# Plain matmuls for tokens 2048 to 2559, masks per key block, and V rows copied on the chip, in a fused attention and MLP kernel

## The chip, the cores and the metric

The kernel runs on one core of one Trainium2 chip. The core has five engines that run side by side: TensorE (PE, matmuls; PEld is its weight load), VectorE (DVE), ScalarE (ACT), GpSimd (POOL, here only a queue that issues DMAs and one iota) and SyncE (SP, a queue for DMAs). They meet through semaphores alone. The metric is the device time of one execution in microseconds; lower is better.

## The reference, cut to what matters

Attention with a sliding window of 32 tokens to each side, for 8 batches, 8 heads, 576 tokens and head size 64. Its output, turned to 4608 tokens by 512 features, goes through a two-layer network with squared ReLU:

```
scores = scale * np.matmul(q, k.transpose(0, 1, 3, 2))
mask = np.abs(pos[:, None] - pos[None, :]) <= 32
scores = np.where(mask, scores, -1e9)
attn = exp(scores - max); attn = attn / sum(attn)
x = (attn @ v).transpose(0, 2, 1, 3).reshape(4608, 512)
h = x @ w_in            # 512 x 2048
g = maximum(h, 0) ** 2
out = g @ w_out         # 2048 x 512
```

## The kernel before, in words

**Attention** works in 24 groups of 192 queries, three for each batch (G = 3 * batch + g). POOL loads q, k and v for a group with casting DMAs (lines 377 and 415). For the first nine groups PE turns q and k (line 463) and DVE or ACT copies the result out (477, 476); for the later ones a transposing DMA on SP does it (491). A group has two key blocks of 128 keys, A and B. For each, PE makes the scores of all heads (531), ACT takes the exponential of 128x1024 (554), DVE multiplies by the 0/1 mask of the window (562), and PE multiplies by V (590), whose 65th column of ones gives the row sum. DVE takes the reciprocal (604) and scales (608) into `xa` and `xb`; the part of the accumulator that block B starts alone is zeroed on ACT (614) or DVE (615). PE (630, 636) or a DMA turns `xa` and `xb` into `xt`.

Key block A of a group begins 32 keys ahead of its 192 tokens, block B 128 later, so the last 64 rows of block B of one group are the first 64 rows of block A of the next group of the batch. The function `load_v` either loads such rows twice, or copies them from one V buffer to the next on DVE (line 410) or ACT (412):

```
if self.vcopy(G) and j == 0:          # vcopy: G % 3 > 0 and G >= VC
    lo += 64
    vs, vf = self.V[(G - 1) % NV][64:128, 1, :, 0:64], vt[0:64, 0, :, 0:64]
    self.p.rec("DVE", lambda e, vs=vs, vf=vf: e.tensor_copy(vf, vs), reads=[("v", (G - 1) % NV, 1)], ...
```

The masks are multiplied for both key blocks in one instruction of 2048 elements where `MP` is 1 and a group's scores were recorded together (groups 6 and up), else for each block in one of 1024. `NPT` is the number of 128x1024 buffers for masked exponentials.

**The first layer** works on tiles of tokens: four of 192, one of 256, then seven of 512 from token 1024 on. A tile of 512 is made in one of two ways. `mm1` is plain: 16 products, each of four matmuls of 128x512 (line 690), then a ReLU from PSUM (665 on ACT, 664 on DVE) and a square (660 on DVE, 659 on ACT) into `gt`. With the tile in `PAIR`, two products share one ReLU and one square of 1024. `mm1s` is Strassen's scheme: seven instead of eight block products, four times 28 matmuls of 128x256 (line 770), with four differences of `xt` (742) ahead of them, and for each quarter a seeding copy in PSUM (809, 810), two copies out (670, 669), two additions (794), a ReLU (800, 801) and squares. A Strassen group may need one more PE matmul that clears its bank (line 895; marked with a w in the second part of `ORDER`, below). `MM1S` lists the tiles made so.

**The second layer** is plain for the first 512 tokens (835) and Strassen's for the rest (line 917, sums on DVE at 885, additions at 949). Outputs leave by DMAs from ACT and SP (847, 848).

**What sets the order.** Every operation is recorded with its reads and writes. A table, `ORDER`, gives each operation its engine and its place: the program is sorted by these numbers and written out, one strict sequence for each engine, with semaphore waits where data crosses engines. A second part of the table gives buffers and PSUM banks. Where PE's sequence has room ahead of token 0's first layer, `fill` puts matmuls on zeros (line 299), which nobody reads.

Of the kernel before, what the change touches and what calls it, by code (L numbers as in the profile page):

```python
# [21 lines left out]
    MM1S=(2048, 2560, 3072, 3584, 4096),  # L22
# [9 lines left out]
    PAIR=(1536,),  # L32
# [9 lines left out]
    MP=1,  # L42
    S34=1,
    NZ=0,
    VC=99,
# [4 lines left out]
    NPT=4,  # L50
# [182 lines left out]
class Gen:  # L233
# [7 lines left out]
    def alloc(self):  # L241
# [733 lines left out]
    def record(self):  # L975
# [81 lines left out]
        at(4.0, self.sums_w2, 4.0)  # L1057
        if cfg["MM1S"]:
            at(4.5, self.sums_w1, 4.5)
# [26 lines left out]
D900 G1350 A129696 D1800 D9508 D10128 D10418 D10688 D7198 D9088 D12405 D8968 D7698 D8398 D9408 D7398 D2020 D9308 D7818  # L1086
D8108 D17412 D9928 D12805 D13710 D7498 D9708 D12605 D17302 D8683 D14866 D23833 D17702 D39949 S900 D4366 S1350 D6598
G1700 G2488 G4852 G4064 G5640 G3276 G8840 G7216 A900 A13271 A1350 A6839 G6428 G9580 G7956 G10464 G11348 G12128 G14580
G15360 G17756 G16140 G12908 G13792 G18536 G19316 P7268 A7873 P8308 A8860 P9765 A10400 D11719 P10190 A11428 D13025
P12475 D13910 D14180 D14966 P15634 D16146 D16416 P15114 P17172 A17612 P10615 D11167 P11225 A12456 P13361 A13996 D15461  # L1090
P13786 A15024 D18507 P16216 D17102 D17822 A18577 P19276 D19746 D20016 P19536 P20851 D21291 P15344 A16867 P14211 A16052
P17665 A19186 D21843 P20426 A21061 D24619 P22598 D23081 D23933 A25450 P26388 D27094 D27364 P24838 P28702 D30325 G20932
G21768 G20096 G16920 G24920 G29504 P41968 D42573 P40496 A41308 P43262 A43897 D45015 P18517 D22528 P43687 A45477 D46595
P19766 A23151 A24140 P45774 D46386 D47280 D48036 P49140 D49610 D49880 P51114 P51344 D51838 P21081 A23646 P23518 D25304
A27788 P26648 A28603 P27308 A29188 D29773 P29592 D34242 G23392 G22604 G27188 G27976 G43361 G45917 P45432 D48531 P47354
A47906 P28042 D34864 A35487 P49400 A50035 D51153 P24178 D25856 P51574 A52352 D53470 P25068 A26479 A29683 P52442 D53127
D54155 D54911 P55806 D56291 D57177 P57386 P58583 D59595 P21913 D23281 D33556 D38025 D37340 D38711 D35969 D45700 D43192
D57862 P22858 A24955 A26974 P25728 D30878 D26409 D32871 D28050 D36654 D28735 D40069 D31430 D32185 P30912 A32202 A32787
P30252 A31122 G26448 G28764 G24180 G25708 G46801 G48521 P47696 D49083 P47986 A49216 P28932 A31707 A36301 P50689 A51324
D52442 P31572 D35417 P51999 A53380 D55406 P44772 A47399 A57337 P55546 D56091 D56491 D58548 P59473 D60148 D60900 P58011  # L1100
P62644 D63084 P36348 D40754 P46034 A46904 A55037 P33960 D39396 P34620 P37008 P38736 P40891 A42229 A59141 P42363 A43233
D50565 P44112 A44982 G45081 G44245 G52653 G47685 G59793 G63781 P57616 A59521 P59733 A60443 P46694 A48721 D64189 P61994
A62994 A64112 D65507 P52702 A55852 P54886 A56842 A62179 P67289 D67759 D68029 A68941 P73039 D73509 D73969 P74079 P75183
A75994 P33096 P35484 P37872 P39632 A40706 A94765 P56066 A58646 P58813 D60348 A61364 P54226 A56347 P56726 A58152 D75340
P60992 D63636 G51029 G42573 G55017 G54229 G58121 G50145 P58241 D59043 P61652 D62204 P32232 P48276 P49825 P53362 A54436
S113850 P76293 A78955 A80051 P65775 A66795 A67913 D69031 P68422 A69549 P71033 D71620 D71890 D72645 P73299 D73769
D74655 P73849 P75413 D75893 P67549 A70240 D70934 P63738 D64821 P64611 A65695 D70249 P60128 P62874 P66425 P69295 A70842
A129316 P71293 A72376 G67125 G57381 G53489 G55805 G65453 G59005 P73559 A74059 P65485 D66725 P74309 A75393 D77130
G56545 G51817 G62945 G49309 G64665 G87303 P75643 A76809 A77927 D79045 S69616 S68326 P70159 A71443 P81919 D82389 D82659
A83760 P84769 D85318 D85588 P103901 P105644 D106314 P72166 A73249 D76445 P77816 A79450 D80263 D86274 D83345 D88177  # L1110
D84100 P85893 P86767 A87851 P89154 P94023 D99960 D95953 A104236 P90288 P91162 D92246 P97154 P98891 A99975 P94897
P102153 D104943 S139197 P101279 P103027 D106866 A116182 P105874 P106748 A107832 A121814 P79543 D80948 A81704 P82179
A85997 P85029 A86689 A95145 G61369 G66337 G60581 G62157 G79875 G75935 P81269 A82732 A84368 D86959 S67036 S71616 P76953
D78026 P90028 D93131 D93401 A94157 P96634 D99005 D99275 S94157 S100030 P83906 A85396 D88863 P80406 D81634 P83043
D89548 A96173 P78679 A80866 P98028 D101178 D101934 G77607 G68701 G69441 G78347 G86419 G104247 P87641 A88501 A89619
D90737 S83639 S91003 P92296 D96638 P92036 D92931 D94087 D95458 P96894 D97364 D97634 S102530 S101280 P95771 A97394
D98319 P88291 A90647 P93159 D94772 D105628 P99765 A103635 P104781 A107159 D108769 G75099 G80759 G84699 G67865 G76819
G100393 P100629 A101489 A102607 D103725 S95407 S92293 P115980 P117103 A118177 A122194 D102619 D116722 D111687 D117608
D112915 P114232 P115106 A116562 P118227 P119101 D120503 A120185 S128302 P121098 P124573 D125657 P122835 P126960
A130126 P127834 P128708 D132956 S140937 P133035 P135657 D136741 S137497 P133909 P134783 A135867 A145085 P108272  # L1120
D109455 D109725 A110480 P111985 D112455 D114133 S112600 S123182 P119975 P121972 D123292 D124580 P112505 P113369
A114442 D121921 G79087 G83911 G83123 G82335 G85535 G107255 P104131 A105013 A106131 D107551 S88423 S96697 P110259
P111122 A112195 A120786 P112245 D112715 D114819 A115574 P117967 D118437 D119322 S115574 S120642 P131309 P132172
A133245 A134363 P108532 P109395 D110469 D131165 G74359 G105775 G81595 G106515 G113703 G108975 P107622 A108839 A111088
D115504 S89713 S111310 P123709 P125447 D128729 D134746 P116843 D117408 D118637 D120008 P120838 D121721 D122606 S119392
S137947 P129582 P130445 A131519 D134060 D132536 D133641 D126840 D135431 P136531 A137178 P138055 D138702 A140576
P138492 D139388 P139820 A141177 P140517 D141869 P142702 D143772 A148131 D155834 P143399 A145465 A150362 P137618
A139974 P140954 A143077 D154996 P142265 A143678 P143836 A144483 P145147 D145794 P145584 D146691 D148062 D149699
P146718 A147530 A151565 P146281 A146928 P148029 A149159 A155866 P150651 D151298 P151348 A152167 P152222 D152939
P153096 D154310 D155415 A156467 P153970 A155264 A160153 P148466 A149761 P151785 A152768 A153460 P152659 D153625  # L1130
P153533 A154663 P155281 D156557 P158116 D159103 D162111 D164054 P159427 A160754 A161446 D128044 D131851 D135851
D140073 D137427 P138946 P141391 A142475 P144273 P147155 D148482 A150964 S154259 P148903 P149777 A154061 P154407
P155718 A158523 P157242 P158553 D159788 S160544 P159864 P161388 D163369 S164124 P162262 P163136 A164220 S190571
G109763 G110599 G90491 G108139 G111435 G134127 P126310 A127170 A128288 D129947 S124432 S125722 P140257 D140759 D141029
A141784 P143139 D144458 D144728 S146733 S145483 G116259 G117047 G117835 G99605 G133243 G140625 P136968 A137828 A138946
D142554 S130042 S128752 P146021 D146491 D147377 D150385 P151088 D151984 D152254 S150563 S153009 G112223 G112963
G105035 G103507 G160271 G141509 P156592 A157495 A159125 D160474 S127012 S121892 P164447 D164917 D165187 A166025
P167766 D168462 D169359 S165943 S185090 D158684 D161692 D162950 D162530 P164010 A164822 P165581 A166633 D180492
P166018 D167091 P167329 A167976 P168026 D168673 P168900 D170044 D172948 A175430 P169774 A170421 A173626 P164707
A165423 P166455 A168578 D176379 P166892 A169781 P169337 A172334 P170648 D173367 P174664 D175693 A177060 D182129  # L1140
P174227 A176458 D187961 P165144 A167234 P168463 A169179 A174829 P170211 A171023 P171085 A171732 P171782 D176798
P176849 D178169 D180073 A181534 P184751 A185398 A186601 P179684 A180331 P181869 A182562 A188976 P182566 A183213
# [80 lines left out]
```

## Time and profile before

| | |
|---|---|
| three runs, median (lowest to highest) | 288.12 us (288.11 to 289.0) |
| the profiled execution: its own time | 288.54 us |
| its span, first to last instruction | 286.7 us |
| busy: PE, PEld, DVE, ACT, POOL | 98%, 81%, 82%, 70%, 41% |
| instructions: PE, DVE, ACT | 3097, 424, 302 |
| moved by DMA | 38.62 MB, 171107 packets |

Busy PE is the union of matmuls in flight. A matmul lasts longer than the next one waits for it, so PE counts as busy while it only runs slower; the time from one matmul's start to the next tells more, and the chain of waits shows it as the length of a run of matmuls. In the page "out<-in" names the tile written and the tile read; "x" is a count.

### The profile page before, as it was taken

The page shows a single profiled execution, that of the slowest core. Times are in us where ns is not written, and L with a number is a line of the kernel's source. Part 1 is how long each engine was busy: PE and PEld are TensorE (multiplying, and loading weights), DVE is VectorE, ACT ScalarE, POOL GpSimd, SP SyncE. Part 2 cuts the span into 40 slices and gives each one's busy share as a digit, 9 for nine tenths or more (in the row PEclk, how much of TensorE's full clock was granted, in tenths as well). Part 3 has the DMA queues.
Part 4 walks back from the last instruction along what each step waited for, and adds up shares of the span by engine and source line. Part 5 has one row for each costly group of instructions (what it writes and reads, how often), then busy time and mean ns, then how long its engine had stood idle before and what let it go on. Part 6 is the DMA issues. An engine that isn't in the chain of part 4 may idle for free.

```text
span 286.7 us, 7639 instructions
## 1 busy us (share of the span) xinstructions
PE 280.1 (98%) x3097; PEld 232.0 (81%) x3115; DVE 236.0 (82%) x424; ACT 201.7 (70%) x302; POOL 117.9 (41%) x153
## 2 busy tenths in 40 slices
PE   8999999999999999999999999999999999999995
PEld 8979858787857775776898898988888888888884
DVE  2779968878898988979889889899999989979631
ACT  1777638887795476636878899888887768776520
POOL 8999109998693269403702994310000000000000
PEclk9999999999999999999999999999999999999999
DMA  9999999999999999999999999998720431102123
GB/s 147 157 192 204 205 161 148 144 158 148 162 141 150 182 148 143 194 163 186 135 195 158 144 162 155 134 189 137 148 53 13 134 87 40 37 2 71 41 91 130
DMA packets 171107, 38.62 MB, mean 135 GB/s; under 512 B 158272, under 2 KB 170560, under 8 KB 171072
## 3 DMA queue, kind: packets, MB, share of 16 engines
q0 software_dynamic: 121920, 18.98, 94.4%
q1 hardware_dynamic: 43344, 14.30, 29.0%
q10 hardware_dynamic: 5808, 4.85, 5.5%
q8 instruction: 25, 0.41, 0.6%
q14 instruction: 10, 0.08, 0.1%
HBM read 38.80 MB, written 9.44 MB: 168 GB/s over the span
## 4 chain that ended last, share of the span: by engine, by line
PE 93%; DVE 3%; ACT 2%; issue 1%; ACTq 0%
PE ps L917 34%; PE ps L770 22%; PE ps L690 19%; PE ps L835 5%; PE ps L590 4%; PE ps L531 4%; PE ps L299 3%; PE ps L463 2%; ACT e L554 1%; PE ps L630 1%; DVE pt L562 1%; PE ps L636 1%; DVE xa L608 0%; ACT oe L670 0%; DVE xb L608 0%
## 5 line engine op out<-in xcount | busy, mean ns | idle before, releaser
L690 PE MATMUL ps<-xt,w 128*128 128x192 bf16 (+2 forms) x438 | 60.9, 286 | 0.7 <-issue 0.3
L670 ACT ACTIVATE oe<-ps 128x512 f32<-128x512 f32 x62 | 36.0, 596 | 29.4 <-PE ps L917 16.6
L554 ACT ACTIVATE e<-ps 128x1024 bf16<-128x1024 f32 x48 | 48.6, 1021 | 11.0 <-PE ps L531 8.9
L665 ACT ACTIVATE rt<-ps 128x512 bf16<-128x512 f32 (+2 forms) x76 | 44.0, 594 | 16.7 <-PE ps L690 9.6
L377 POOL DMA_DIRECT2D raw<-in_k_dram x46 | 36.4, 810 | 35.9 <-DMA kq<-raw 21.7
L690 PEld LDWEIGHTS ps<-xt,w 128*128 128x128 bf16 x448 | 38.7, 98 | 13.8 <-DVE xt L646 0.3
L377 POOL DMA_DIRECT2D raw<-in_q_dram x46 | 36.9, 815 | 27.3 <-DMA kq<-raw 26.5
L917 PE MATMUL ps<-w,gt 128*128 128x256 bf16 x384 | 47.3, 273 | 0.0
L659 ACT ACTIVATE gt<-rt 128x512 bf16<-128x512 bf16 (+2 forms) x56 | 43.2, 793 | 2.6 <-DVE rt L664 1.8
L415 POOL DMA_DIRECT2D v<-in_v_dram x48 | 42.0, 887 | 6.1 <-PE ps L590 6.1
L917 PEld LDWEIGHTS ps<-w,gt 128*128 128x128 bf16 x384 | 36.8, 98 | 6.0 <-issue 0.6
L562 DVE TENSOR_TENSOR pt<-e,mask 128x2048 bf16<-128x2048 bf16 (+1 forms) x30 | 30.3, 1009 | 3.9 <-ACT e L554 3.5
L770 PE MATMUL ps<-xs,sw 128*128 128x256 bf16 x240 | 32.7, 272 | 0.0
L917 PE MATMUL ps<-ts,gt 128*128 128x256 bf16 x256 | 31.7, 273 | 0.0
L917 PE MATMUL ps<-ts,ss 128*128 128x256 bf16 x256 | 31.4, 273 | 0.0
L794 DVE TENSOR_TENSOR rt<-ps,oe 128x512 bf16<-128x512 f32 x40 | 27.3, 687 | 4.0 <-PE ps L770 3.2
L917 PEld LDWEIGHTS ps<-ts,ss 128*128 128x128 bf16 x256 | 24.4, 98 | 3.7
L917 PEld LDWEIGHTS ps<-ts,gt 128*128 128x128 bf16 x256 | 24.7, 98 | 3.1
L770 PEld LDWEIGHTS ps<-xs,sw 128*128 128x128 bf16 x240 | 23.0, 98 | 2.6
L660 DVE TENSOR_TENSOR gt<-rt 128x1024 bf16<-128x1024 bf16 (+2 forms) x40 | 23.3, 590 | 0.5 <-ACT rt L665 0.4
L770 PE MATMUL ps<-xt,w 128*128 128x256 bf16 x160 | 22.1, 273 | 0.1
L664 DVE TENSOR_SCALAR rt<-ps 128x512 bf16<-128x512 f32 (+2 forms) x28 | 19.0, 685 | 2.1 <-PE ps L690 1.3
(69 smaller groups left out, 389.9 us busy)
## 6 DMA issues: line engine op xcount, KB each, us to landing
out_dram<-oe SPq DMA_DIRECT2D x19, 256.0 KB, 3.0
out_dram<-oe ACTq DMA_DIRECT2D x17, 256.0 KB, 2.5
v<-in_v_dram POOLq DMA_DIRECT2D x32, 128.0 KB, 5.7
w<-in_moe_w_in_dram POOLq DMA_DIRECT2D x4, 512.0 KB, 9.6
w<-in_moe_w_out_dram POOLq DMA_DIRECT2D x4, 512.0 KB, 16.7
raw<-in_q_dram POOLq DMA_DIRECT2D x18, 96.0 KB, 5.3
raw<-in_q_dram POOLq DMA_DIRECT2D x14, 112.0 KB, 4.9
raw<-in_k_dram POOLq DMA_DIRECT2D x14, 112.0 KB, 4.6
```

The lines of the kernel that those rows point to most:

```text
L377: self.p.rec("POOL", lambda e, j=j, dst=dst: e.dma_start(dst, s[j]), writes=[self.rtag(t, b, g, j)], dma=(f"{t}{G % self.cfg['NRAW']}{j}", ...
L415: self.p.rec("POOL", lambda e, j=j, lo=lo, hi=hi, k0=k0: e.dma_start(vt[lo - k0:hi - k0, j, :, 0:64], self.v[b, :, lo:hi, :].rearrange("h ...
L554: last = self.p.rec("ACT", lambda e, ef=ef, v=v: e.activation(ef(), self.bank(v, 0, 2), ACTF.Exp, scale=0.125), reads=[v], writes=tags, ke ...
L562: self.p.rec("DVE", lambda e, pf=pf, ef=ef, mb=mb, n=n: e.tensor_tensor(pf(y=0, n=n), ef(y=0, n=n).rearrange("p (w h q) -> p w h q", w=n, ...
L659: alt = ("ACT", act(c), lambda e: e.activation(dst, src(), ACTF.Square)) if self.cfg["ALT"] else None
L660: self.p.rec("DVE", lambda e: e.tensor_tensor(dst, src(), src(), ALU.mult), reads=rd, writes=wr, key=key, dur=dve(c), name=name, alt=alt, ...
L665: return self.p.rec("ACT", lambda e: e.activation(dst(), src(), ACTF.Relu), reads=rd, writes=wr, key=key, dur=act(c), name=name, alt=alt, ...
L670: self.p.rec("ACT", lambda e: e.activation(dst(), src(), ACTF.Copy), reads=rd, writes=wr, key=key, dur=act(c), name=name, alt=alt, bias=se ...
L690: mm = e.matmul(ht[:, n * x:n * x + n], self.W1[:, ft, 128 * d:128 * d + 128], self.XT[:, ft, r:r + n], start=(ft == 0 and x == 0), stop=( ...
L770: mm = e.matmul(bk[:, 256 * x:256 * x + 256], lhs(k, 256 * m + 128 * x), rhs[:, k, :], start=start and x == 0 and k == 0, stop=(k == 1), s ...
L794: add.append(p.rec("DVE", lambda e: e.tensor_tensor(hs(), src(), self.oe(u), ALU.add), reads=[tg, u], writes=[(hh, y)], key=kk, dur=dve(51 ...
L917: mm = e.matmul(op[:, 256 * y:256 * y + 256], lhs[:, l0[0] + k, a:a + 128], rhs[:, r0 + k, c0:c0 + 256], start=start and y == 0 and k == 0 ...
```

## The change

Five settings change, and with them the whole table `ORDER`:

```diff
-    MM1S=(2048, 2560, 3072, 3584, 4096),
+    MM1S=(2560, 3072, 3584, 4096),
...
-    PAIR=(1536,),
+    PAIR=(),
...
-    MP=1,
+    MP=0,
...
-    VC=99,
+    VC=0,
...
-    NPT=4,
+    NPT=3,
...
 ORDER = """
-D900 G1350 A129696 D1800 D9508 D10128 D10418 D10688 D7198 D9088 D12405 D8968 D7698 D8398 D9408 D7398 D2020 D9308 D7818
+D900 G1350 A131953 D1800 D9496 D10301 D10591 D11011 D2305 D9981 D12979 D2505 D8173 D9696 D10201 D9396 D7888 D19226
...
```

Tokens 2048 to 2559 leave Strassen's scheme: 112 matmuls of 128x256 go, 64 of 128x512 come. Tokens 1536 to 2047 take one ReLU for each product. The 18 masks of 2048 become 36 of 1024. Sixteen groups (all that are not the first of their batch) get the first 64 rows of key block A by a copy on the chip, ten on DVE and six on ACT; 16 of the 32 V loads of 128 rows become loads of 64. One buffer for masked exponentials goes, and one of the two bank-clearing matmuls.

On DVE, at the start of the program, the rows from the scaling of the first group's block A (`xa0`) to that of the second group's (`xa1`). Before:

```order
L608 TENSOR_TENSOR xa0<-ps,rs0 64x512 [waits s_DVE]
L345 MEMSET v3 128x16x2
L615 MEMSET ps 64x2x260 [waits s_DVE]
L562 TENSOR_TENSOR pt<-e,mask 128x1024 [waits s_ACT]
L604 RECIPROCAL rs1<-ps 128x8 [waits s_PE]
L608 TENSOR_TENSOR xb0<-ps,rs1 128x512 [waits s_DVE]
L604 RECIPROCAL rs2<-ps 64x8 [waits s_PE]
L329 MEMSET mask 32x64
L293 MEMSET xa2 64x256
L293 MEMSET kq1 128x4x16
L608 TENSOR_TENSOR xa1<-ps,rs2 64x512 [waits s_DVE]
```

The same stretch of DVE in the changed kernel; `d_v01` is the landing of the V load from which the copy reads:

```order
L608 TENSOR_TENSOR xa0<-ps,rs0 64x512 [waits s_DVE]
L562 TENSOR_TENSOR pt<-e,mask 128x1024 [waits s_DVE,s_ACT]
L562 TENSOR_TENSOR pt<-e,mask 128x1024 [waits s_ACT]
L410 COPY v1<-v0 64x8x64 [waits d_v01]
L604 RECIPROCAL rs1<-ps 128x8 [waits s_PE]
L608 TENSOR_TENSOR xb0<-ps,rs1 128x512 [waits s_DVE]
L604 RECIPROCAL rs2<-ps 64x8 [waits s_PE]
L608 TENSOR_TENSOR xa1<-ps,rs2 64x512 [waits s_DVE]
```

The zeroing of PSUM went to ACT, four memsets went elsewhere, one mask that stood ahead of this stretch came in, and the first V copy stands between the masks and the reciprocal.

On PE, where the second batch begins, the turns of its first k and q (128x112), the first scores (531) and what stands around them. Before:

```order
L835 MATMUL ps<-w,gt 128x512 x16
L463 MATMUL ps<-ident,raw 128x112 x8
L835 MATMUL ps<-w,gt 128x512 x4
L463 MATMUL ps<-ident,raw 128x112 x8
L690 MATMUL ps<-xt,w 128x192 x8
L531 MATMUL ps<-kq 128x128 x16
L690 MATMUL ps<-xt,w 128x192 x16
```

The same place on PE in the changed kernel:

```order
L690 MATMUL ps<-xt,w 128x192 x16
L463 MATMUL ps<-ident,raw 128x112 x8
L690 MATMUL ps<-xt,w 128x192 x8
L463 MATMUL ps<-ident,raw 128x112 x8
L690 MATMUL ps<-xt,w 128x192 x16
L531 MATMUL ps<-kq 128x128 x8
L835 MATMUL ps<-w,gt 128x512 x8
```

The scores come apart into single blocks, and between the second turn and the first scores stand sixteen matmuls of 128x192 where eight stood.

On PE, the beginning of tokens 2048 to 2559. Before, with Strassen's products of the first layer at line 770:

```order
L917 MATMUL ps<-w,gt 128x256 x8
L770 MATMUL ps<-xt,w 128x256 x4
L531 MATMUL ps<-kq 128x128 x16
L770 MATMUL ps<-xt,w 128x256 x8
L770 MATMUL ps<-xs,sw 128x256 x4
L917 MATMUL ps<-w,gt 128x256 x8
L770 MATMUL ps<-xs,sw 128x256 x4
L590 MATMUL ps<-v,pt 128x65 x8
```

The beginning of the same tokens on PE in the changed kernel:

```order
L917 MATMUL ps<-ts,gt 128x256 x8
L690 MATMUL ps<-xt,w 128x512 x8
L531 MATMUL ps<-kq 128x128 x16
L917 MATMUL ps<-w,gt 128x256 x8
L690 MATMUL ps<-xt,w 128x512 x12
L590 MATMUL ps<-v,pt 128x65 x8
L690 MATMUL ps<-xt,w 128x512 x4
L917 MATMUL ps<-w,gt 128x256 x8
```

Plain products of 128x512 stand where the Strassen products stood, mixed with the same second-layer products (917), scores and V products.

More of the change, by code (lines that the diff above doesn't have):

```diff
@@ L1091 @@
[L1091 to L1105, printed above, removed]
@@ new lines @@
+P152548 D153875 D155030 S167444 S170536 P152808 A153881 A162216 D155716 D157553 D160029 D164165 P166821 A167633
+P168829 A169476 D170884 P168392 D170199 P170577 A171281 P172325 D173259 P172762 D176005 D182112 D182951 P178089
+D179842 A186974 P167258 A168234 P169266 A170078 A175633 P169703 A170679 P171014 A171882 P171451 D172574 P173199
+D173945 D175586 D179087 P173636 A174430 D182531 P167955 A168836 P171888 A172535 A173227 P170140 A173828 P174333
+A175031 P174770 D176690 P176081 D177446 A178901 D180528 P177652 A178299 A188177 P180924 A181571 P182495 A183802
@@ new lines @@
+A187575 P183806 A184453 P185117 A185764 P185554 D186456 P186865 D188735 D189840 A190673 P188436 A189380 A190071
+D161819 D162794 D164585 D168295 D168981 P175207 P176518 A177602 P180050 P181361 D185207 A183201 S183892 P178526
+P182932 A185055 P184243 P185991 A188778 P187302 P188873 D190259 A199741 P189747 P192145 D196209 A197557 P191271
+P193669 D196895 A200729 G115945 G123133 G127025 G115109 G153272 G151504 P149026 A149886 D151004 A150914 D152375
+S137173 S131019 P152288 D154075 D154345 A155346 P156272 D157353 D159343 S173036 S176866 G118357 G127861 G125449
@@ new lines @@
+G124661 D162504 G161604 G152388 P157406 A158266 D161133 A159294 D160448 S138463 S144099 P164813 D165283 D165553
+A166328 P167695 D171303 D171573 S171786 S179406 G150024 G163920 G150764 G158548 A176842 G157856 G169532 P160667
+A165300 D167610 A164272 D166924 S155577 S169246 D187827 D188316 D189421 D191145 P194543 A195190 P196745 A197937
+A206129 P197182 A199140 P199190 D199907 P200064 D201277 P200938 D202648 A205101 D207017 P202249 A203061 D205912
+P197879 A198538 P199627 D201963 A209895 P200501 A201148 P202718 D203365 P203415 D204251 P205163 D206331 D207702
@@ new lines @@
+D210980 P206297 A207332 A225747 P203852 A204499 P205600 A206730 A211707 P206734 A207933 P208045 A208692 P208919
+D210295 P210667 D211666 D213753 A214962 P211541 A212910 A215990 P208482 A209294 P210230 A212308 D213334 P211104
+D212648 P213112 A213759 P213549 D215277 P215734 D217357 D219148 A219756 P216171 A217098 D227552 D187141 D200592
+D192249 D197580 D193620 P194997 P195871 A196955 P198316 P201375 D208121 A202459 A203662 P204289 P209356 A210497
+P207171 P212238 A214361 P213986 P214860 D215963 A216718 P219006 P219880 D226866 S227622 P217258 P218132 A220784
@@ L1190 @@
+0 5 4 1 6 1 6 0 3 5 2 5 2 3 2 0 4 3 1 2 3 0 4 2 0 1 1 2 4 2 1 2 0 0 0 1 1 4 3 0 0w 1 0 2 4 7 2 6 5 4 2 1 6 0 3 2 2 7 4
+6 5 4 4 7 6 3 1 5 0 4 2 0 4 0 1 1 0 0 3 0 4 2 1 0 0 2 4 2 1 6 0 0 4 4 0 0 1 1 5 6 3 2 7 0 4 4 2 4 6 1 5 2 1 4 1 0 5 4
+1 2 6 0 5 1 3 2 5
 """
```

158 lines of the change are left out of this document (75 added, 83 removed), and 11 rows, old and new, of the table ORDER.

## The prediction

> **What bounds the kernel now.** I read the page first: busy shares and the 40 slices.
>
> ```profile
> span 286.7 us, 7639 instructions
> PE 280.1 (98%) x3097; PEld 232.0 (81%) x3115; DVE 236.0 (82%) x424; ACT 201.7 (70%) x302; POOL 117.9 (41%) x153
> PE   8999999999999999999999999999999999999995
> PEclk9999999999999999999999999999999999999999
> ```
>
> PE is busy from the first slice to the last, at the full granted clock. Then I asked what PE waits for, and how much of each stretch it is busy (the windows; the columns are PE, PEld, DVE, ACT, POOL, each with its count).
>
> ```profile
> PE ps L299 <- DVE zz L293: 1.2, 1, 1.2
> PE ps L590 <- ACT e L554: 0.4, 1, 0.4
> PE ps L690 <- issue: 0.3, 2, 0.2
> PE ps L590 <- ACT ps L614: 0.2, 1, 0.2
> PE ps L835 <- issue: 0.2, 1, 0.2
> ```
>
> ```profile
> 0.00:20.00 20.00, 18.46 (x297) 17.04 (x298) 11.89 (x43) 11.94 (x15) 19.05 (x29) 1.00 1.63 164
> 40.00:60.00 20.00, 19.24 (x286) 15.89 (x287) 15.06 (x29) 16.23 (x25) 17.06 (x22) 1.00 2.25 146
> 60.00:140.00 80.00, 79.05 (x812) 56.57 (x821) 68.48 (x110) 53.06 (x69) 46.54 (x60) 1.00 1.76 160
> 140.00:260.00 120.00, 119.89 (x1288) 105.46 (x1288) 108.70 (x189) 98.50 (x158) 25.37 (x32) 1.00 0.96 111
> 260.00:286.70 26.70, 23.47 (x216) 20.73 (x213) 13.52 (x20) 10.36 (x18) 0.00 (x0) 1.00 0.26 90
> ```
>
> Apart from the start, PE's waits that have a name come to 1.1 us. The windows give the room that is left: 0.76 us without a matmul in 40 to 60, 0.95 in 60 to 140, 0.11 in 140 to 260. So the change moves the time by PE's own work, by the start (where most of PE's time goes to matmuls on zeros), and by these small gaps. What it saves on DVE, ACT or in DMA counts only where PE waits for it.
>
> **The change part by part: PE's work.** The chain of waits gives the pace, since a run of matmuls in it has the length that the next one waited for.
>
> ```profile
> 113.02 1.73 PE ps L690 x8
> 246.79 8.73 PE ps L770 x80
> ```
>
> The 128x512 runs at 1.73 / 8 = 0.216 us, the 128x256 at 8.73 / 80 = 0.109. The plain tile costs 64 x 0.216 = 13.82 us, Strassen's 112 x 0.109 = 12.22: **+1.6 us**. One bank-clearing matmul of 128x512 goes: **-0.22**. Both bounds are close, since nothing else in the chain is so regular.
>
> The Trainium skill speaks to this in "TensorE: Matmul & The Clock Gate", section "Back-to-back issue gap": it gives 131 ns for a matmul of 512 columns in a sustained stream and 81 for 128, and calls 216 the isolated figure. This trace has 216 in a stream, so it does not agree; by that rule the plain tile would cost 8.4 us, which is a rival below.
>
> **The start.** Until the first layer begins, PE follows DVE.
>
> ```profile
> 8.47 0.56 PE ps L299 x10
> 14.03 0.69 DVE xa L608
> 15.06 0.49 DVE ps L615
> 17.55 0.11 DVE mask L329
> 17.77 0.27 DVE xa L293
> 18.05 0.09 DVE kq L293
> 18.15 0.71 DVE xa L608
> L562 DVE TENSOR_TENSOR pt<-e,mask 128x1024 bf16<-128x1024 bf16 x12 | 8.3, 691 | 1.7 <-ACT e L554 1.4
> L394 DVE CAST raw<-ts 112x512 bf16<-112x512 f32 x2 | 0.9, 428 | 4.2 <-DMA ts<-in_k_dram 4.2
> L664 DVE TENSOR_SCALAR rt<-ps 128x512 bf16<-128x512 f32 x13 | 8.9, 687 | 1.3 <-PE ps L690 0.7 <-ACT e L554 0.3
> ```
>
> Between the two scalings (14.03 to 18.15) the change takes out the zeroing and three memsets, 0.49 + 0.11 + 0.27 + 0.09 = 0.96 us, and puts in a V copy. No copy from SBUF to SBUF stands in the trace; the nearest row is the cast of 512 elements, 0.43, and a read from PSUM, 0.69, bounds it above. Net -0.53 (-0.27 at the upper bound). The mask that comes in (0.69) stood just ahead of this stretch before, so it moves the first scaling forward by as much. A second reading: the program carries 148 matmuls on zeros where it carried 161, and ten take 0.56, so 13 fewer are 0.73 us of room that the new order does not have. I take **-0.7**, with bounds 0 (the DVE chain is not what ends last) and -1.0 (all that goes, and the copy is hidden). The cover for the first copy is the V load: it must have landed when DVE arrives.
>
> **Where the second batch begins.**
>
> ```profile
> 42.57 0.64 DVE kq L477
> 46.04 1.32 PE ps L690 x16
> 51.47 1.03 ACT e L554
> ```
>
> The first scores of batch 1 waited for the copy of the turned k (0.64), with eight matmuls of 128x192 between them and the turn; now sixteen stand there, 1.32 us, which covers the copy. The exponential at 51.47 stood in the chain because a V product (590) had only scores (531) just ahead of it; in the changed order second-layer matmuls (835) stand there. Together they make the 0.76 of this window: I take **-0.5**, bounds 0 and -0.76. To hide this the changed order needs the loads of k and q of batch 1 earlier than before; they share POOL's queue with the weights, and if one lands late the wait comes back here.
>
> **Late stretched runs.**
>
> ```profile
> 174.82 0.91 PE ps L770 x8
> 197.51 2.34 PE ps L770 x20
> 205.22 0.60 PE ps L770 x4
> ```
>
> At 0.109 these should take 0.87, 2.18 and 0.44: 0.36 us together, in products that waited for DVE or ACT to empty a bank while PE counted as busy. The order there is new; I take **-0.3**, bounds 0 and -0.4.
>
> **Masks, pairs, copies, buffers.**
>
> ```profile
> L562 DVE TENSOR_TENSOR pt<-e,mask 128x2048 bf16<-128x2048 bf16 x18 | 22.0, 1221 | 2.2 <-ACT e L554 2.1
> L794 DVE TENSOR_TENSOR rt<-ps,oe 128x512 bf16<-128x512 f32 x40 | 27.3, 687 | 4.0 <-PE ps L770 3.2
> L665 ACT ACTIVATE rt<-ps 128x1024 bf16<-128x1024 f32 x5 | 5.1, 1023 | 5.9 <-PE ps L690 5.9
> ```
>
> Masks: 18 x (2 x 0.691 - 1.221) = +2.9 us of DVE. Copies: ten on DVE, 4.3 at 0.43, six on ACT. Strassen's eight additions go, 8 x 0.687 = -5.5, and some ReLUs move over from ACT. DVE comes out about even and stays near 82%, ACT near 70% (a ReLU of 1024 takes 1.023, two of 512 a little more); PE's matmuls hide all this. If that cover is gone, each instruction costs PE its own length, 0.4 to 0.7. With three buffers for masked exponentials instead of four, a mask may wait for the V product of three blocks earlier: nothing, unless PE is late. The sixteen shorter V loads relieve DMA, and no wait of PE above is for a DMA: nothing.
>
> What is new is a wait of DVE and ACT for a landing, in the middle of the program.
>
> ```profile
> POOL raw L377 <- DMA kq<-raw: 48.2, 8, 13.8
> L415 POOL DMA_DIRECT2D v<-in_v_dram x4: 777/849/930, 106.6 to 112.9; - x4
> DMA to landing us min/median/max: 4.3/5.2/6.2
> L377 POOL DMA_DIRECT2D raw<-in_k_dram x8: 721/833/872, 105.2 to 116.1; - x8
> DMA to landing us min/median/max: 4.2/5.5/7.2
> ```
>
> The four rows after the first are the V loads and the k and q loads of 105 to 120, a burst of issues after POOL had waited for buffers (48.2 us in eight such waits). In it a landing takes 4.2 to 7.2 us. Behind a held copy stand, on DVE, the mask of the next block and the reciprocals and scalings, and on ACT exponentials and ReLUs; PE waits for those with V products and free banks. The 24 groups hand work over between ACT, DVE and PE now at a cost to PE of 0.4 + 0.2 us, about 0.025 for a group; sixteen copies at half that are **+0.2**, bounds 0 and +1.4 (below).
>
> The Trainium skill has a rule against such copies: "SBUF — State Buffer", section "Who interferes with whom", says that a DVE copy with both ends in SBUF can enter a mode in which GpSimd is locked out until it ends, and the descriptors of POOL's DMAs are written by GpSimd. No run here shows it; in the burst above POOL issues a V load in 0.78 to 0.93 us with DVE 86% busy (68.48 of the 80 us around).
>
> Even a POOL held for ten copies of 0.43 us loses 4.3 of the 48.2 us that it waits anyhow, so I count nothing for that.
>
> **Sum.** +1.6 - 0.22 - 0.7 - 0.5 - 0.3 + 0.2 = +0.1 us, on a profiled execution of 288.54 (span 286.7 and 1.84 around it). That run lies 0.4 above the median, 288.12, of which two runs lie within 0.01; the terms are differences, so they go onto the median: **288.2 us**. A measurement here tells about 0.3%, 0.86 us, from no change.
>
> **The rivals.** *A V copy holds DVE or ACT.* A copy that meets a landing of 7.2 instead of 5.2 us holds its engine by up to 2.0 us; a bank that is emptied in 0.69 lets PE run on for about that long. Two held copies of which 0.7 us each reaches PE give +1.4, 289.6. It decides from the second such copy on. For it: DVE is 82% busy and strictly in order, and the loads come in bursts. Against it: there are five V buffers, and V loads ran ahead of use far enough that PE waited for none. Chance 0.18.
>
> *The gaps stay.* If the start and the small gaps are latencies that any order has, only the sum of work counts: 288.12 + 1.6 - 0.22 + 0.2 = 289.7. For it: 0.95 us of gaps in 60 to 140 are spread over many handovers. Against it: the two at 43 and 52 have names, and what named them moved. Chance 0.12.
>
> *The gaps all close.* Start -1.0, second batch -0.76, late -0.4, half of the 0.95 as well, no new wait: 1.6 - 0.22 - 2.6 = -1.3, 286.8. For it: masks of one block let the first V product start 0.53 us earlier (1.221 - 0.691) in every group. Chance 0.11.
>
> *Wide matmuls come cheaper than narrow ones.* With 512 columns at a pace well under 216 ns, say 131, and 256 at 98 (between 81 and 131), the tile would cost 8.4 against 11.0, -2.6 instead of +1.6: 284.0. The page on TensorE would have it so; the chain's runs speak against it. Chance 0.02.
>
> *The change doesn't do what it says:* the V rows are saved, but PE did not wait for them. That is part of the forecast, not a case beside it.
>
> **How the numbers follow.** The forecast, within 0.3% of before, has 0.57; the two slower rivals 0.30 together, the two faster 0.13. The forecast's own range is 287.3 to 289.0. To leave out no more than 2 in 10, the range goes up to 289.7, which takes in both slower rivals at their price, and down to 287.2: the faster rivals, 0.13, stay outside, and so does what is slower than priced.
>
> **What the changed profile would show.** The first layer's first matmul (690) some 0.6 us earlier than before; no DVE copy of a turned k in the chain near 43; runs of 690 at 0.216 in tokens 2048 to 2559, without gaps; DVE and ACT without a wait for a V load, or with short ones that no PE wait follows. I would be wrong if DVE shows waits of 1 us or more for V loads (first rival), if the windows 40 to 60 and 60 to 140 still lack 1.5 us together (second), or if the end comes late by something not in this list.

## The result, and the profile after

The changed kernel takes 289.17 us, the median of 15 runs from 288.0 to 290.47; before takes 288.11 us (15 runs, 287.7 to 289.0). The ratio is 1.0039, with a 95% interval of 1.0028 to 1.005. The forecast was 288.2 us, no change that can be told; the result lies inside the range, but 1.0 us above the forecast and past the 0.3%, 0.86 us, that the prediction took for no change. The profiled execution of the changed kernel is the slowest of its runs, 290.47 us, so its waits need not be the typical ones.

The head of its page, the waits of PE that are discussed below, and the windows:

```profile
span 288.7 us, 7534 instructions
PE 280.1 (97%) x3034; PEld 225.4 (78%) x3053; DVE 236.9 (82%) x444; ACT 201.4 (70%) x300; POOL 114.6 (40%) x153
```

```profile
PE ps L531 <- ACT rt L801: 1.2, 1, 1.2
PE ps L690 <- DMA w<-in_moe_w_in_dram: 1.0, 1, 1.0
PE ps L590 <- DMA v<-in_v_dram: 0.2, 1, 0.2
```

```profile
0.00:20.00 20.00, 18.57 (x304) 16.58 (x305) 13.05 (x42) 13.17 (x17) 19.06 (x29) 1.00 1.59 166
20.00:40.00 20.00, 18.83 (x235) 16.80 (x236) 15.73 (x36) 11.49 (x20) 16.47 (x23) 1.00 1.68 187
40.00:60.00 20.00, 19.84 (x252) 14.48 (x254) 17.70 (x34) 16.46 (x25) 11.74 (x16) 1.00 2.14 150
60.00:140.00 80.00, 79.07 (x796) 54.57 (x804) 69.05 (x121) 58.53 (x82) 45.88 (x60) 1.00 1.81 158
140.00:260.00 120.00, 118.51 (x1228) 100.52 (x1230) 104.34 (x189) 93.26 (x147) 21.44 (x28) 1.00 0.83 101
```

The engines are as busy as forecast: DVE 82%, ACT 70%. The stretch 40 to 60, where 0.76 us was missing, now lacks 0.16. But 20 to 40 lacks 1.17 us and 140 to 260 lacks 1.49, where there had been almost nothing (0.11 in 140 to 260; 20 to 40 of before is the row below), and PE has two waits of about 1 us that were not there.

```profile
20.00:40.00 20.00, 19.95 (x217) 16.32 (x215) 18.39 (x36) 11.60 (x19) 9.85 (x13) 1.00 1.51 195
```

Not every missing tenth is a wait: where the chain of waits shows a run of seven matmuls instead of eight, a record is lost, and such losses look like gaps in the windows. A window with fewer matmuls than weight loads on record, such as 796 against 804 in 60 to 140, is a sign of it.

**The first wait, at 20 us**, is read from the weight loads for line 690 (of before, then of after; behind the three durations stand the starts of the first and the last) and from the chain of waits of after.

```profile
L690 PEld LDWEIGHTS ps<-xt,w x448: 95/98/99, 18.6 to 133.1; 128*128 128x128 bf16 x150
```

```profile
L690 PEld LDWEIGHTS ps<-xt,w x512: 95/98/102, 17.7 to 161.3; 128*128 128x128 bf16 x171
```

```profile
9.91 0.75 POOL w L431
10.66 0.87 POOL v L415
11.53 9.69 DMA w<-in_moe_w_in_dram
21.22 0.14 issue
21.36 2.72 PE ps L690 x31
```

The first layer begins 0.9 us earlier, somewhat more than the forecast said. Then it runs into the second quarter of `w_in`, which POOL issued at 11.5 and which landed at 21.2. By the trace of before the same quarter landed at 21.0, and nobody waited, because PE came to it later. The size of this wait differs from execution to execution: in four other profiles below, in which the loads and the order of the start are the same, it is 0.23 us, 0.49 us, and twice none, where PE had already waited 0.64 and 0.68 us for a k. So 1.0 us is not its typical size.

**The second wait, at 181 us**, goes by one name in the list and by another in the order of time. The chain, then DVE's and PE's timelines (in square brackets the idle time ahead and what ended it), then SP's timeline and its transposes of `xb` between 150 and 185 with their times from issue to landing:

```profile
179.34 0.39 ACT rt L665
179.96 1.06 ACT rt L801
181.03 0.81 issue
181.84 0.62 PE ps L531 x16
```

```profile
181.05 0.69 DVE L608 TENSOR_TENSOR xb<-ps,rs 128x512 bf16<-128x512 f32 x1 [1.80 <-DMA xt<-xb]
181.84 0.62 PE L531 MATMUL ps<-kq 64*128 64x128 bf16 x16 [1.23 <-ACT rt L801]
```

```profile
165.12 3.29 SPq L848 DMA_DIRECT2D out_dram<-oe  x2
171.82 1.36 SPq L652 DMA_TRANSPOSE xt<-xb  x1
```

```profile
DMA to landing us min/median/max: 2.5/4.4/9.1
```

The list puts PE's wait down to a ReLU on ACT. That ReLU ended at 181.03, and PE went on 0.81 us later, 0.1 us after DVE's scaling at 181.05 had ended; the "issue" of 0.81 in the chain is where that scaling belongs: in the program these scores wait for exactly this scaling. The scaling writes group 19's block B into a buffer from which a transposing DMA of group 16 still had to read: DVE idled 1.80 us for that DMA. SP had issued it at 171.8, behind two stores that were held for their results, a transpose of `xa`, and a transpose of k or q that was held for its load, though its data had been ready since about 157. It landed 9.1 us after its issue, beside the last of POOL's burst of loads (issued from 150.7 to 172.2).

The V copies and the masks by group (busy us, mean ns, idle time ahead of them), and the DVE copies by duration (lowest, median, highest, then the starts of the first and the last):

```profile
L410 DVE COPY v<-v 64x512 bf16<-64x512 bf16 x10 | 3.8, 385 | 0.2
L412 ACT ACTIVATE v<-v 64x512 bf16<-64x512 bf16 x6 | 3.7, 621 | 0.0
L562 DVE TENSOR_TENSOR pt<-e,mask 128x1024 bf16<-128x1024 bf16 x48 | 32.2, 687 | 3.2 <-ACT e L554 1.9 <-PE ps L590 0.8
```

```profile
L410 DVE COPY v<-v x10: 289/290/636, 15.1 to 219.3; 64x512 bf16<-64x512 bf16 x10
```

Ahead of the copies DVE idled 0.2 us in all and ACT not at all: no copy was held by a landing. The ten DVE copies take 0.29 or 0.48 to 0.64 us, 0.385 in the mean; the four longer ones, at 20.4, 118.9, 127.2 and 163.1, each ran while POOL was issuing a load, and of the other six only the one at 15.1 did. The masks wait for ACT and for PE, 3.2 us in 48.

### The profile page after: what moved, and what is told of

The parts are those of the page before. It is cut to its first block, busy times and chain, and to the rows that moved or that the text cites. A ratio compares the mean times of both kernels' runs of the same rounds, so it can differ in the third digit from the quotient of the medians.

```text
span 288.7 us, 7534 instructions
## 1 busy us (share of the span) xinstructions
PE 280.1 (97%) x3034; PEld 225.4 (78%) x3053; DVE 236.9 (82%) x444; ACT 201.4 (70%) x300; POOL 114.6 (40%) x153
## 4 chain that ended last, share of the span: by engine, by line
PE 80%; DMA 7%; POOL 7%; issue 3%; ACT 1%; DVE 1%; SPq 1%; POOLq 0%; DVEq 0%; ACTq 0%
PE ps L917 29%; PE ps L690 19%; PE ps L770 17%; PE ps L835 5%; POOL raw L377 4%; PE ps L531 4%; PE ps L590 3%; DMA w<-in_moe_w_in_dram 3%; DMA v<-in_v_dram 2%; POOL v L415 2%; DMA kq<-raw 2%; PE ps L463 1%; PE ps L636 1%; PE ps L630 1%; DVE oe L669 0%
## 5 line engine op out<-in xcount | busy, mean ns | idle before, releaser
L690 PE MATMUL ps<-xt,w 128*128 128x192 bf16 (+2 forms) x500 | 75.0, 297 | 1.8 <-DMA w<-in_moe_w_in_dram 1.0
L690 PEld LDWEIGHTS ps<-xt,w 128*128 128x128 bf16 x512 | 44.3, 98 | 20.2 <-ACT xt L644 1.1
L665 ACT ACTIVATE rt<-ps 128x512 bf16<-128x512 f32 (+1 forms) x85 | 47.2, 571 | 15.3 <-PE ps L690 12.1
L670 ACT ACTIVATE oe<-ps 128x512 f32<-128x512 f32 x50 | 29.1, 596 | 23.9 <-DVE gt L885 10.0
L659 ACT ACTIVATE gt<-rt 128x1024 bf16<-128x1024 bf16 (+2 forms) x47 | 39.7, 862 | 5.2 <-DVE rt L664 4.8
L562 DVE TENSOR_TENSOR pt<-e,mask 128x1024 bf16<-128x1024 bf16 x48 | 32.2, 687 | 3.2 <-ACT e L554 1.9
L664 DVE TENSOR_SCALAR rt<-ps 128x512 bf16<-128x512 f32 (+1 forms) x35 | 22.2, 637 | 5.0 <-PE ps L690 3.5
L770 PE MATMUL ps<-xs,sw 128*128 128x256 bf16 x192 | 25.9, 273 | 0.0
L794 DVE TENSOR_TENSOR rt<-ps,oe 128x512 bf16<-128x512 f32 x32 | 21.5, 686 | 2.3 <-ACT oe L670 1.3
L590 PEld LDWEIGHTS ps<-v,pt 128*128 128x128 bf16 x384 | 17.4, 98 | 3.5 <-issue 0.4
```

The lines of the kernel that those rows point to most:

```text
L562: self.p.rec("DVE", lambda e, pf=pf, ef=ef, mb=mb, n=n: e.tensor_tensor(pf(y=0, n=n), ef(y=0, n=n).rearrange("p (w h q) -> p w h q", w=n, ...
L590: mm = e.matmul(ps[z:z + n, c:c + 65], ptt[:, 4 * (h % 2) + h // 2, z:z + n], vt[:, w, h, 0:65], start=((w == 0 or (z == 64 and split)) an ...
L659: alt = ("ACT", act(c), lambda e: e.activation(dst, src(), ACTF.Square)) if self.cfg["ALT"] else None
L665: return self.p.rec("ACT", lambda e: e.activation(dst(), src(), ACTF.Relu), reads=rd, writes=wr, key=key, dur=act(c), name=name, alt=alt, ...
L670: self.p.rec("ACT", lambda e: e.activation(dst(), src(), ACTF.Copy), reads=rd, writes=wr, key=key, dur=act(c), name=name, alt=alt, bias=se ...
L690: mm = e.matmul(ht[:, n * x:n * x + n], self.W1[:, ft, 128 * d:128 * d + 128], self.XT[:, ft, r:r + n], start=(ft == 0 and x == 0), stop=( ...
```

## The experiments

My theory after the first comparison: PE's work and the closed gaps are as forecast, and what is late is a few landings in the new order, above all the one at 181. The rivals: the V copies cost it, or the split masks do. All ratios are against the kernel before on the same chip, 288.17 to 288.20 us.

**Moving loads out of the way.** The first edit changes POOL's order alone: group 13's V load goes ahead of its burst, and four later V loads go to the end of POOL's last burst.

```diff
-G120769
+G114000
...
-G165496
+G177800
...
-G162296
+G177000
...
-G167216 G168744
+G178600 G179400
```

> The changed kernel with five V loads moved on POOL's queue: that of group 13's block B ahead of its burst, four of groups 21 to 23 (used after 200 us) to the end of theirs. Theory 'late landings': PE's waits at 128 (0.3 us) and 181 us (1.5 us in the profiled run, less in others) go, since the transposes that DVE waits for land earlier; about 288.4, ratio to before 1.001. Rival 'V copies hold DVE or ACT' and rival 'the gaps stay, PE's work counts': nothing changes, 289.2, ratio 1.004.

Measured: 289.15 us (288.27 to 290.63), ratio 1.0038, interval 1.0023 to 1.0054. Nothing gained: the 288.4 expected for late landings did not come, and by its time alone the run agrees with the rivals. The waits of PE and of DVE show why:

```profile
PE ps L531 <- issue: 1.4, 1, 1.4
PE ps L463 <- DMA raw<-in_k_dram: 0.6, 1, 0.6
DVE xb L608 <- DMA xt<-xb: 2.0, 1, 2.0
```

The wait for V at 128 is gone and the one at 181 is as long as before. A place in an order holds back nothing on a queue that has no reason to wait: POOL issued the four loads right behind the others, and the transpose of `xb` took 10.0 us to land.

**Halving the second quarter of the weights**, so that its first half lands earlier, with the two groups of products that use it exchanged in PE's order, so that each waits for its own half.

```diff
-    W1H=(),
+    W1H=(1,),
```

> The changed kernel with the second quarter of the first layer's weights loaded in two halves, and the two products that use it in PE's order exchanged so that each waits for its own half. Late landings: PE's wait of 1.0 us at 20 us falls to about 0.4, 288.6, ratio 1.002. Both rivals: 289.2, ratio 1.004.

Measured: 289.35 us (288.31 to 291.0), ratio 1.0041, interval 1.0026 to 1.0055. The wait for the weights is gone, but the median has not fallen:

```profile
PE ps L531 <- ACT rt L801: 0.6, 1, 0.6
PE ps L463 <- DMA raw<-in_k_dram: 0.3, 1, 0.3
```

A wait for k stands at the start instead. In this profile the run of 56 first-layer matmuls that had waited for the weights still begins 0.86 us earlier, at 20.50 instead of 21.36. But the 0.96 us of that one run are not the typical wait, and the end of one of 0.2 to 0.5 us cannot be told from nothing in medians of 12 and 15 runs.

**Both together.**

> Both edits above together. Late landings: 287.8, ratio 0.999, no wait of PE for a landing left above 0.5 us. Both rivals: 289.2, ratio 1.004.

Measured: 289.23 us (288.4 to 289.65), ratio 1.0033, interval 1.002 to 1.0046: a miss as well. At 181 PE still waits 1.1 us.

**Without the V copies**: the rows are loaded twice again, with everything else in the order of the changed kernel.

```diff
-    VC=0,
+    VC=99,
```

> The changed kernel without the sixteen V copies: all V rows are loaded, in the changed order. 'V copies hold DVE or ACT': 288.0, ratio 0.9995. Late landings: the loads are longer again, so the waits for landings at 20, 128 and 181 us are the same or longer, 289.2 to 290, ratio 1.004 to 1.007. 'The gaps stay': 289.2, ratio 1.004.

Measured: 291.93 us (290.37 to 293.81), ratio 1.0136, interval 1.0102 to 1.017. That is 2.8 us slower than with the copies, and more than the 289.2 to 290 expected for late landings. The edit takes away the copies and makes the loads longer at once, so it gives only the balance of the two: in this order copies with shorter loads gain. The wait at 181 does not come from the copies: without them DVE again waits 1.8 us for the same transpose, and 1.0 us for one of `xa`. POOL's queue (packets, MB, and the time of the packets as a share of 16 engines' span), of the changed kernel and of this one:

```profile
q0 software_dynamic: 113728, 17.93, 89.7%
```

```profile
q0 software_dynamic: 121920, 18.98, 95.1%
```

The median time from issue to landing of a V load of 128 rows goes from 5.6 to 6.2 us, that of a turn of `xb` from 3.7 to 4.5. How these later landings add up to 2.8 us was not traced one by one.

**Only the transpose of `xb`.** In SP's order group 16's transpose of `xb` goes ahead of the two stores; nothing else moves on any engine.

```diff
-S167444 S170536
+S167444 S156500
```

> The changed kernel with one transposing DMA (xt from xb1, group 16) issued some 14 us earlier on SP's queue, ahead of two stores; nothing else. 'One late transpose': DVE's wait for it at 180 us and PE's wait of 1.4 us behind it go, and the time falls by 1.2 to 1.4 us to 287.9, ratio to before 0.999. 'Queue in general' (any transpose of this burst comes late, another takes its place): 288.8 or more, ratio 1.002 to 1.004.

Measured: 288.41 us (288.13 to 288.93), ratio 1.0007, interval 0.9996 to 1.0018. This one place takes back 0.76 of the 1.06 us, less than the 1.2 to 1.4 expected, which were the waits of single profiled runs. Its waits of PE (that at the program's very start left out), two of its windows, from SP's timeline the issue of the moved transpose, and from PE's the matmuls behind the wait for the weights:

```profile
PE ps L690 <- DMA w<-in_moe_w_in_dram: 0.2, 1, 0.2
PE ps L463 <- DMA raw<-in_k_dram: 0.2, 1, 0.2
```

```profile
60.00:140.00 80.00, 80.00 (x808) 54.89 (x805) 69.07 (x121) 58.68 (x82) 45.03 (x59) 1.00 1.90 160
140.00:260.00 120.00, 120.00 (x1244) 101.62 (x1242) 105.88 (x192) 94.37 (x149) 21.39 (x28) 1.00 0.75 99
```

```profile
157.00 1.26 SPq L652 DMA_TRANSPOSE xt<-xb  x1
```

```profile
20.61 4.78 PE L690 MATMUL ps<-xt,w 128*128 128x192 bf16 x56 [0.23 <-DMA w<-in_moe_w_in_dram]
```

Issued at 157 instead of 172, the transpose landed long before DVE came, and from 60 to 260 us PE is never without a matmul.

**The same with group 13's V load ahead of its burst.**

> The edit above, and the V load of group 13's block B ahead of its burst, so that PE's V product at 128 us does not wait for it (0.25 us in three of five profiles). 'One late transpose': 287.6, ratio 0.998. 'Queue in general': 288.6 or more.

Measured: 288.25 us (287.8 to 289.48), ratio 0.9999, interval 0.998 to 1.0017. The 287.6 expected did not come; the step of 0.16 us from the kernel above is inside the uncertainty of both.

**All three repairs**: the transpose, the V load, and the weights in two halves.

> The changed kernel with three repairs at once: the transposing DMA of group 16's xb ahead of two stores, the V load of group 13 (the one that landed at 128 us) ahead of its burst, and the second quarter of w_in loaded in two halves with the two products that need the second half made later. Theory (each late landing costs PE what its wait shows: 1.0 at the start, 0.2 at 128, 1.2 at 180): 289.2 less 2.4 is 286.8 to 287.3 us, ratio 0.996, faster than before. Rival (the start is bounded by all of the first loads together, and one that comes earlier makes another later, as the halves alone showed): nothing is gained over the kernel without the halves, 288.25 us, ratio 1.000.

Measured: 288.25 us (287.75 to 288.75), ratio 1.0003, interval 0.9994 to 1.0012. The rival's time came out, but the profile does not show its reason. At the start nothing replaced the wait for the weights: the run of 56 matmuls begins at 20.31, 0.3 us earlier than with the moved transpose alone, and 20 to 40 is full. What came is a wait late in the program, at 179.9:

```profile
PE ps L531 <- DMA kq<-raw: 0.6, 1, 0.6
140.00:260.00 120.00, 119.42 (x1237) 101.05 (x1236) 105.30 (x191) 93.81 (x149) 21.39 (x28) 1.00 0.80 99
```

The scores that had waited behind the transpose of `xb` now wait for a transposed k or q, another DMA of SP's queue in the same burst. This is one profile, of a run of 288.55 us; that the start is bounded by all of its first loads together was not shown.

**The masks by themselves**, in the kernel before.

```diff
-    MP=1,
+    MP=0,
```

> The kernel before with each mask of 2048 elements split into two of 1024 at the same place in DVE's order; nothing else. Prediction's reading (hidden by PE): DVE +2.9 us busy, time 288.1 to 288.4, ratio 1.000 to 1.001. If DVE's length reaches PE: 18 x 0.15 us, up to 290.9, ratio 1.010.

Measured: 288.11 us (287.84 to 288.99), ratio 0.9996, interval 0.9984 to 1.0009. The split masks cost nothing there.

**The V copies by themselves**, in the kernel before: twelve groups, all on DVE, each copy just ahead of the group's first mask.

```diff
-    VC=99,
+    VC=0,
...
-        return G % 3 > 0 and G >= self.cfg["VC"]
+        return G in (2, 4, 8, 11, 13, 14, 16, 17, 19, 20, 22, 23)
```

> The kernel before with twelve of the sixteen V copies, all on DVE just ahead of the group's first mask, and the shorter loads for them; order otherwise as before. Prediction's reading (hidden, loads not waited for): 288.1 to 288.4, ratio 1.000 to 1.001. 'V copies hold DVE': 289 or more, ratio 1.003. 'Shorter loads matter' (from the run without copies, which was 2.8 us slower than the changed kernel): 287.5 or less, ratio 0.998.

Measured: 289.41 us (289.2 to 289.89), ratio 1.004, interval 1.0026 to 1.0053. So there the copies do cost 1.2 us, about a third of their own length (twelve of 0.29 us or more), although they shorten the loads and DVE waits for no V load. PE has waits in this profile that before has not, 0.26 us at 23.0, 0.30 at 117.6 and 0.24 at 169.2, each within 3 us of a copy (21.8, 115.9 and 166.6). The prediction's reading was wrong here, and two readings were left: the copies' own length, or something about the loads.

**Twice the copying.** Ahead of eleven of the twelve copies stand two more, of half the size, into a scratch tile.

```diff
+                for i in range(2 if G < 23 else 0):
+                    self.p.rec("DVE", lambda e, i=i, vs=vs: e.tensor_copy(self.VX[:], vs[:, 4 * i:4 * i + 4]),
+                               reads=[("v", (G - 1) % NV, 1)], writes=["vx"], key=key + 2, dur=200, name=f"vd{b}{g}{i}")
```

> The kernel before with twelve V copies on DVE (289.41 us), and ahead of eleven of them two more copies of half their size into a scratch tile, so about twice the time of DVE for copying, with the same shorter V loads and the same place in the order. Theory A (a copy just ahead of the mask delays the V product and PE by its own length): the cost above before, 1.2 us, grows to about 2.4, 290.6 us, ratio 1.008. Theory B (the cost comes from the loads, from the landing that the copy waits for or from what the shorter loads change in the queues): no more than 0.3 us is added, 289.4 to 289.7, ratio 1.004 to 1.005.

Measured: 293.75 us (293.25 to 294.19), ratio 1.0195, interval 1.0182 to 1.0208: 4.3 us more than with single copies. Theory B is out. Theory A has the right cause, DVE's time, but not the size: it said 1.2 us more. The added copies, and the chain of waits around one of them (lines from 253 on are shifted by one to four in this kernel: 414 is the V copy, 566 the mask, 889 a sum of the second layer, 668 a ReLU, 558 the exponential):

```profile
L412 DVE COPY vx<-v x22: 221/222/585, 21.7 to 231.5; 64x256 bf16<-64x256 bf16 x22
```

```profile
79.43 0.69 DVE rt L668
80.15 0.46 DVE vx L412
80.64 0.22 DVE vx L412
80.86 0.20 DVE v L414
81.09 0.88 DVE pt L566
82.23 0.60 DVE ss L889
82.84 0.69 DVE rt L668
```

Here the chain that ends last runs through the copies and the mask behind them, on DVE, where in the kernel before, and in that with single copies, no row of DVE stands in the chain between 60 and 140 us. 22 copies of 0.22 us or more are 4.9 us or more, and 4.3 of them reach the end.

**Less work for PE.** The kernel with the moved transpose, with the fourth of four contraction steps left out for tokens 2048 to 2559, so that part of the first layer of these tokens is missing.

```diff
-                    for ft in range(4):
+                    for ft in range(3 if t0 == 2048 else 4):
...
-                                      start=(ft == 0 and x == 0), stop=(ft == 3), skip_group_check=True)
+                                      start=(ft == 0 and x == 0), stop=(ft == (2 if t0 == 2048 else 3)), skip_group_check=True)
```

> The changed kernel with the transposing DMA of group 16's xb moved ahead of two stores, and with the fourth of four contraction steps left out for tokens 2048 to 2559: 16 matmuls of 128x512 fewer, part of the first layer of these tokens is not computed. Theory (PE's own work sets the time, a 128x512 counts 0.216 us): 16 x 0.216 = 3.46 us less than the 288.41 us of the kernel with the moved transpose alone, so 284.95 us, ratio 0.989. Rival (in this stretch DVE and ACT, which empty the banks, are the bound and PE's matmuls are only stretched over it): less than half of it comes out, 287 us or more.

Measured: 287.09 us (285.6 to 289.37), ratio 0.9976, interval 0.9955 to 0.9998. Of 3.46 us of matmuls 1.3 us come out, so the theory fell. PE's timeline at the end of the tile, without the change to the tile and then with it:

```profile
159.87 1.03 PE L690 MATMUL ps<-xt,w 128*128 128x512 bf16 x4
160.83 0.62 PE L531 MATMUL ps<-kq 64*128 64x128 bf16 x16
```

```profile
157.65 0.81 PE L690 MATMUL ps<-xt,w 128*128 128x512 bf16 x3
159.56 0.62 PE L531 MATMUL ps<-kq 64*128 64x128 bf16 x16 [1.09 <-ACT rt L665]
```

At the tile's last product PE is 2.2 us ahead, 157.65 against 159.87. Then it waits 1.1 us until ACT has emptied a bank, and it ends 1.1 us ahead (spans of 285.2 and 286.3). A part of what is missing is not the edit's: in this run a k landed late at the start, and PE waited for it 0.68 us instead of 0.20. So ACT stands close behind PE at this place, and a gain of 3.5 us in the tile does not pass whole; how much would pass without the late k was not measured.

## Why the prediction was right or wrong

**PE's work, +1.6 and -0.22: the pace held, and the sum agrees.** In the changed kernel the plain tile runs at the length that was taken, 1.73 / 8 = 0.216 us for a matmul:

```profile
154.05 1.73 PE ps L690 x8
```

The rival in which wide matmuls come cheaper is gone: it gave 284.0. The Trainium skill's 131 ns ("TensorE: Matmul & The Clock Gate", section "Back-to-back issue gap") does not agree with this stream either: by that rule the eight would have taken 1.05 us. That PE's work alone sets the time was not shown; in the kernel with less of it PE waits for ACT before the gain is through.

**The sum without the late transpose.** With that one transfer moved, the kernel takes 288.41 us, +0.2 against before, where the sum of the forecast was +0.1. That agreement is partly luck, since single terms were off in both directions. The second batch gave -0.76 and not -0.5, and the wait priced at +0.2 for V loads never came; with +1.38 for PE's work, about -0.4 is then left for the start and the late runs, for which -1.0 was taken. This is an estimate, and the medians behind it tell no more than some 0.3 us.

**The start, -0.7: the step that failed is its cover.** The first matmul of the first layer came 0.9 us earlier, a little more than the sum over DVE's rows said. But the cover was named as the V load alone, and the sentence that no wait of PE is for a DMA was taken to mean that DMA would not matter. A landing at 21 us, for which nobody waits, becomes the bound as soon as PE arrives a microsecond sooner. What was left of the 0.9 us differs from run to run: the wait took 0.96 of it in the profile of the changed kernel, 0.23 in that with the moved transpose. The medians of two kernels without this wait are no lower than those of their partners with it, so what the term is worth in the total stays open, between 0 and what was taken.

**Where the second batch begins, -0.5: right.** The window 40 to 60 went from 19.24 to 19.84 us of PE, 20.00 in the kernel with the moved transpose, so all of the 0.76, the end of the bounds, came in this window. Neither the copy of a turned k nor an exponential stands in the chain there any more.

**Late stretched runs, -0.3: right place, wrong question.** I asked what the old order lost there and assumed that a new one would lose less. In its place came the wait at 181. The prediction named nothing that could be late in that stretch; the "something not in this list" that would make it wrong is what happened.

**The new wait, +0.2: a wait of DVE for a landing came, but not for V.** None of the copies waited for its load. What DVE waited for was a transposing DMA that still read the buffer which DVE was to write. I had priced the landings of POOL's loads, 4.2 to 7.2 us in a burst, and not those of SP's transposes beside the burst, 9.1 us. The queue in front of that transpose (two stores and two more transposes) was also there to be read in the changed order. In the kernel before the same kind of transfer had a longest landing of 6.1 us in the same part of the program, and nobody waited for it; over the whole program its longest was 8.5, so the price could have been read before the change. This is the main cause: 0.76 of 1.06 us. What remains against before, 0.2 us, has an interval that takes in 0 (ratio 0.9996 to 1.0018), and is not explained further.

**Shorter V loads, "nothing": wrong.** In the new order loading the rows twice costs 2.8 us, even with the work of the copies gone. That no wait of PE is for a DMA describes the old order; it does not say how much later the landings may come.

**Masks hidden: right**, 0.9996 on their own, in the order of before. The unpaired ReLUs and the missing buffer, also put at nothing, were not tested by themselves.

**The copies hidden by PE's matmuls: it depends on the place.** In the changed kernel they wait for nothing and are a little shorter than estimated, 0.385 us on DVE in the mean instead of 0.43. In the kernel before, just ahead of a mask, they cost 1.2 us, and more of them cost nearly their full length. The prediction gave the price for when the cover is gone, each instruction its own length; the added copies show nearly that, the first twelve about a third of it. So the cover is not DVE's 18% of idle time but, as I read it, the lead that DVE has at that point; that lead was not measured place by place.

**The rivals.** "A V copy holds DVE or ACT" by a late landing: no such wait in the changed kernel. "The gaps stay": no, the window 40 to 60 is full with the transpose moved. The 0.95 us in 60 to 140 was misread as room: before has 812 matmuls on record there against 821 weight loads, and the same order with split masks shows 80.00 of 80 us, so most of it was lost records. "The gaps all close": with the repairs they nearly do, and the time is still 288.25, not 286.8; most of the 0.95, of which it counted half, was never there, and a wait of 0.6 came at 180. On the rule that a DVE copy locks GpSimd out (the Trainium skill, "SBUF — State Buffer", section "Who interferes with whom"): POOL's V issues took 0.69 to 1.05 us after and 0.77 to 1.10 before, so no slowing of POOL is seen. What is seen is the other side: the DVE copies of 0.48 to 0.64 us instead of 0.29 all stand where POOL was issuing.

## What to carry to other kernels

When an edit makes the bound engine arrive earlier, list the landings just behind the old arrival: a transfer that nobody waits for today may be the next bound, and "no wait is for a DMA" is no price for one. In a remade order look at every buffer that a queued DMA still reads, and at what stands ahead of that DMA on its queue; moving one transpose ahead of two held stores was worth three quarters of the loss. An instruction on an engine with idle time is free only where that engine has a lead, and the busy share does not tell where: DVE was busy 82% of the time in the kernel in which twelve copies then cost 1.2 us. And the waits of one profiled run are no prices for the median of many.

## What was not expected of the hardware

A transposing DMA of `xb` took 2.5 us from issue to landing at best and 9.1 beside a burst of POOL's loads (10.0 in the kernel with five V loads moved). A copy of 64x512 on DVE took 0.29 us, and 0.48 to 0.64 in four of the five cases in which POOL was issuing a load at the same time. The spread from run to run is no sure sign of a landing on the path: it went from 2.5 us (288.0 to 290.47) to 0.8 (288.13 to 288.93) when one transpose was moved, but it is 1.7 us (287.8 to 289.48) with that transpose and one V load moved, and the kernel before, measured beside these two, spread over 2.8 us (287.81 to 290.6).
